# First gate and value of block 0 on three batches ahead of the fourth's output, with two loads reordered and one split

## Chip, cores, metric

One core of a Trainium2 chip. The metric is the device time of one execution in microseconds (us), the median over the executions. On one core the state is read from the times alone: slow is over 1.5% above the fastest of the same kernel, and no execution used here was. The kernel before takes 226.5 us; the change is a fine one, and everything it touches lies in the first 36 us.

## The reference, cut to what matters

```python
for b in range(nb):                       # attention in blocks, decay lam per head
    intra = einsum('bhic,bhjc->bhij', qb, kb) * Dmask
    out[:, :, sl] = einsum('bhij,bhjd->bhid', intra, vb) + einsum('bhid,bhde->bhie', qb * lam_pow, kv_state)
    kv_state = lam_block * kv_state + einsum('bhsd,bhse->bhde', kb * rev_pow, vb)
x = out.transpose(0, 2, 1, 3).reshape(B * S, H * D)          # 3072 x 512
y = (sigmoid(x @ w_gate) * (x @ w_val)) @ w_out              # d_ff 1536
```

Four batches, eight heads, 768 positions, head size 64. The kernel takes 128 positions of all four batches as one block (six blocks) and splits `d_ff` into twelve units of 128.

## The kernel before: the parts concerned

`XT` is the attention output of a block, transposed, as the input of the gate and the value. `load_w(W, src, i, w)` loads columns `i*w` to `(i+1)*w`; `GW` is 256, so `GW // 2` is one unit's slice. All loads here cast from float32 to bf16 and are issued on the POOL queue.

```python
    load(0, "v", 2, 3)
    load_w(WG, wg_r, 0, GW // 2)
    load(0, "v", 3, 4)
    load_w(WV, wv_r, 0, GW // 2)
    load_w(WG, wg_r, 1, GW // 2)
    load_w(WV, wv_r, 1, GW // 2)
    # ... (cut)
    load_gv(1, GW)                  # gate and value slices of units 2 and 3
    load_gv(2, GW)
    # ... (cut: block 0's transposes, scores, masks)
    piece_a0(1)                     # output of batch 1 into XT
    idle(2)                         # two matmuls of zeros, filler
    piece_a0(2)
    idle(2)
    g0 = psum()
    mm_part(g0, WG, 0, 0, 0, 3 * C)           # gate of unit 0 on three batches
    piece_a0(3, True)
    make_kd0(1, nc.vector)
    v0 = psum()
    mm_part(v0, WV, 0, 0, 0, 3 * C)
    mm_part(g0, WG, 0, 0, 3 * C, TCH)         # ... on the fourth
    sigm(0, 0, g0)
    mm_part(v0, WV, 0, 0, 3 * C, TCH)
    prod(0, 0, v0)
    # ... (cut) unit 1, with c(0, 0) between its gate and its value, c(0, 1) after it
    # ... units 2 and 3: both gates, both values; 4: gate, value; then 5 to 8
    t(1, 0)                         # block 1's first transposes: tq, then tk
    gv(0, 9)
    sc(1, 0)                        # block 1's first scores
```

## Time and profile before

| | before |
|---|---|
| time | 226.52 us (226.45 to 226.9) at first, 226.57 with three more executions |
| PE busy | 97% of the span of 224.5 us |
| PE idle from 36 to 222 us | 0.38 us |
| start of the first gate, end of its three-batch part | 14.68, about 15.33 us |
| start of unit 2's gate | 19.54 us |
| block 1's first `tk` transposes, last `k` load landed | 32.09, 32.07 us |

To read such a kernel, ask first where the bounding engine is not dense, then what it waits for there. A matmul busy share hides filler matmuls (the two at 13.94 us count as 0.61 us of busy time).

### The profile page before, as it was taken

Reading aid. Unit: us, or ns where it says so; the run is one execution under the profiler, and the core shown is the slowest. Engines: PE = TensorE matmul, PEld = TensorE weight load, DVE = VectorE, ACT = ScalarE, POOL = GpSimd, SP = SyncE. Lnnn points to the kernel's source line nnn. Section 1 sums busy time; section 2 is a strip of 40 time slices with the busy share of each in tenths; the row PEclk is TensorE's granted clock in tenths of the full one; section 3 lists DMA queues with packets and bytes.
Section 4 is the critical chain, followed back from the end, with each engine's and each line's share of the span. In section 5 each row is a group of like instructions: output and inputs, shape, how many; then the busy total and the mean of one; then the engine's idle time right before and its main releaser. Section 6 shows DMA issues by size and latency. Waiting matters only on the chain.

```text
span 224.5 us, 4265 instructions
## 1 busy us (share of the span) xinstructions
PE 218.5 (97%) x1748; PEld 114.6 (51%) x1748; DVE 105.5 (47%) x192; ACT 79.6 (35%) x150; POOL 78.4 (35%) x77
## 2 busy tenths in 40 slices
PE   7799999999999999999999999999999999999994
PEld 2454455888854454444445444446444445444443
DVE  7796847595530713336732445742335840333300
ACT  5664334435422234333225333115333225333221
POOL 8995698983691008930006940000000000000000
PEclk9999999999999999999999999999999999999999
DMA  6999999999999992999021999021920012100022
GB/s 109 155 173 194 189 176 156 157 194 166 157 198 184 217 178 83 204 156 108 1 96 55 230 145 133 1 96 47 176 62 0 0 53 91 47 3 0 0 93 95
DMA packets 105891, 25.70 MB, mean 114 GB/s; under 512 B 96016, under 2 KB 102928, under 8 KB 105872
## 3 DMA queue, kind: packets, MB, share of 16 engines
q0 software_dynamic: 81264, 13.90, 80.0%
q1 hardware_dynamic: 23568, 11.28, 19.7%
q10 hardware_dynamic: 1040, 0.26, 0.5%
q8 instruction: 13, 0.21, 0.4%
q14 instruction: 6, 0.05, 0.1%
HBM read 28.32 MB, written 6.29 MB: 154 GB/s over the span
## 4 chain that ended last, share of the span: by engine, by line
PE 94%; DMA 3%; DVE 1%; issue 1%; ACT 1%; POOLq 0%
PE po L478 27%; PE gp L415 21%; PE vp L421 21%; PE gp L450 5%; PE gp L429 5%; PE vp L456 5%; PE op L312 3%; PE sp L299 3%; DMA kb<-in_k_dram 3%; PE op L324 1%; PE cp L399 1%; PE po L467 1%; DVE MT L202 1%; PE tk L238 0%; ACT XT L352 0%
## 5 line engine op out<-in xcount | busy, mean ns | idle before, releaser
L424 DVE TENSOR_TENSOR ht<-sg,vp 128x512 bf16<-128x512 bf16 x54 | 37.1, 687 | 64.0 <-PE vp L421 63.9
L478 PE MATMUL po<-WO,ht 128*128 128x512 bf16 x276 | 62.0, 380 | 0.0
L415 PE MATMUL gp<-XT,WG 128*128 128x512 bf16 x216 | 55.5, 380 | 0.0
L421 PE MATMUL vp<-XT,WV 128*128 128x512 bf16 x216 | 55.4, 379 | 0.0
L418 ACT ACTIVATE sg<-gp 128x512 bf16<-128x512 f32 x54 | 32.2, 597 | 59.0 <-PE gp L415 59.0
L478 PEld LDWEIGHTS <-ht 128*128 128x128 bf16 x276 | 26.3, 98 | 31.0
L421 PEld LDWEIGHTS <-WV 128*128 128x128 bf16 x216 | 21.1, 98 | 25.5
L415 PEld LDWEIGHTS <-WG 128*128 128x128 bf16 x216 | 20.8, 98 | 24.7
L481 ACT COPY ob<-po 128x512 f32<-128x512 f32 x23 | 13.5, 585 | 52.3 <-PE po L478 50.4
L204 DVE TENSOR_TENSOR MT<-sp,mask 128x512 bf16<-128x512 f32 x40 | 25.2, 683 | 10.1 <-PE sp L299 10.1
L382 POOL TENSOR_TENSOR sd<-Sb,dec 128x512 f32<-128x512 bf16 x8 | 8.1, 1037 | 42.0 <-DVE Sb L406 42.0
L450 PE MATMUL gp<-XT,WG 128*128 128x256 bf16 x96 | 14.4, 273 | 0.0
L456 PE MATMUL vp<-XT,WV 128*128 128x256 bf16 x96 | 14.4, 273 | 0.0
L460 DVE TENSOR_TENSOR ht<-sg,vp 128x256 bf16<-128x256 bf16 x24 | 10.0, 420 | 8.6 <-PE vp L456 8.6
L453 ACT ACTIVATE sg<-gp 128x256 bf16<-128x256 f32 x24 | 9.2, 383 | 13.0 <-PE gp L450 11.9
L91 POOL DMA_DIRECT2D vb<-in_v_dram x10 | 12.8, 1281 | 0.8 <-DMA WG<-in_moe_w_gate_dram 0.6
L373 POOL TENSOR_TENSOR kd<-kb,kds 128x1024 bf16<-128x1024 bf16 x6 | 11.3, 1904 | 4.1 <-DMA kb<-in_k_dram 4.1
L406 DVE TENSOR_TENSOR Sb<-cp,sd 128x512 bf16<-128x512 f32 x8 | 5.2, 686 | 15.4 <-PE cp L399 15.4
L339 ACT CAST XT<-op 128x512 bf16<-128x512 f32 x19 | 9.9, 598 | 2.1 <-PE op L312 2.0
L450 PEld LDWEIGHTS <-WG 128*128 128x128 bf16 x96 | 9.2, 98 | 1.8 <-issue 0.2
L456 PEld LDWEIGHTS <-WV 128*128 128x128 bf16 x96 | 9.4, 98 | 1.1
L77 POOL DMA_DIRECT2D qb<-in_q_dram x8 | 9.4, 1184 | 0.0
(79 smaller groups left out, 161.7 us busy)
## 6 DMA issues: line engine op xcount, KB each, us to landing
out_dram<-ob SPq DMA_DIRECT2D x21, 256.0 KB, 2.1
kb<-in_k_dram POOLq DMA_DIRECT2D x10, 256.0 KB, 8.7
qb<-in_q_dram POOLq DMA_DIRECT2D x8, 256.0 KB, 8.3
vb<-in_v_dram POOLq DMA_DIRECT2D x4, 512.0 KB, 13.2
WO<-in_moe_w_out_dram POOLq DMA_DIRECT2D x3, 512.0 KB, 8.6
WG<-in_moe_w_gate_dram POOLq DMA_DIRECT2D x5, 256.0 KB, 8.5
WV<-in_moe_w_val_dram POOLq DMA_DIRECT2D x5, 256.0 KB, 9.0
qb<-in_q_dram POOLq DMA_DIRECT2D x6, 128.0 KB, 8.3
```

The source lines that it names most:

```text
L91: nc.gpsimd.dma_start(out=lst[n][:, b0:b1], in_=src[b0:b1, :, sl, :].rearrange("b h s d -> s (b h) d"))
L204: nc.vector.tensor_tensor(out=out.rearrange("p (e x) c -> p e x c", e=2), in0=x.rearrange("p (e x) c -> p e x c", e=2), in1=mask.rearrange ...
L373: nc.gpsimd.tensor_tensor(out=KD[n][:, e], in0=K[n][:, e], in1=kds[:, e::2].unsqueeze(1).unsqueeze(3).to_broadcast([128, B, HP, D]), op=AL ...
L415: nc.tensor.matmul(gp, lhsT=WG[:, mt, fs], rhs=x[:, mt, :], start=(mt == 0), stop=(mt == NMT - 1))
L418: nc.scalar.activation(sg, gp, AF.Sigmoid)
L421: nc.tensor.matmul(vp, lhsT=WV[:, mt, fs], rhs=x[:, mt, :], start=(mt == 0), stop=(mt == NMT - 1))
L424: nc.vector.tensor_mul(HT[n, ft], sg, vp)
L429: nc.tensor.matmul(ps[:, lo:hi], lhsT=W[:, mt, ft * 128:(ft + 1) * 128], rhs=x[:, mt, lo:hi], start=(mt == 0), stop=(mt == NMT - 1))
L450: nc.tensor.matmul(gp[:, cs], lhsT=WG[:, mt, fs], rhs=x[:, mt, cs], start=(mt == 0), stop=(mt == NMT - 1))
L456: nc.tensor.matmul(vp[:, cs], lhsT=WV[:, mt, fs], rhs=x[:, mt, cs], start=(mt == 0), stop=(mt == NMT - 1))
L478: nc.tensor.matmul(po, lhsT=HT[n, ft][:, tt * 128:(tt + 1) * 128], rhs=WO[:, ft, :], start=(ft == 0), stop=(ft == NFT - 1))
L481: nc.scalar.copy(ob, po)
```

## The change

The intent is to have PE do the gate and the value of unit 0 on three batches while the fourth batch's output is still on its way, instead of filler; to have the value slice there in time; to put the state product c(0,0) where PE waits for the copies of batch 3; and to have unit 2's gate slice land sooner, because PE would arrive at it sooner.

```diff
     load_w(WG, wg_r, 0, GW // 2)
+    load_w(WV, wv_r, 0, GW // 2)
     load(0, "v", 3, 4)
-    load_w(WV, wv_r, 0, GW // 2)
 ... piece_tk0: for the first pair of batches a PSUM tile per batch; each copy right after its four transposes
-        tk = ps_at.tile([128, 2, 2, 2 * C], BF16, name="tk", tag="ps")
 ...
+            if i == 0 or bp == 0:
+                tk = ps_at.tile([128, 1 + bp, 2, 2 * C], BF16, name="tk", tag="ps")
+            x = tk[:, i if bp else 0]
+            (four transposes into x)
+            nc.scalar.copy(KS[0, bp][:, :, i].rearrange("p e x c -> p e (x c)"), x)
 ... c(n, pair): for block 0 the copy of the state is put off
-                nc.vector.tensor_copy(dst, cp)
+                CP[bp] = cp                       # keep(bp) copies it later
 ...
-    load_gv(1, GW)
+    load_w(WG, wg_r, 2, GW // 2)
+    load_w(WG, wg_r, 3, GW // 2)
+    load_w(WV, wv_r, 1, GW)
     load_gv(2, GW)
 ...
-    piece_a0(2)
-    idle(2)
+    piece_a0(2, (nc.scalar.copy, nc.scalar.copy))     # two halves, two tiles
     g0 = psum()
     mm_part(g0, WG, 0, 0, 0, 3 * C)
-    piece_a0(3, True)
-    make_kd0(1, nc.vector)
     v0 = psum()
     mm_part(v0, WV, 0, 0, 0, 3 * C)
+    piece_a0(3, (nc.scalar.copy, nc.vector.tensor_copy))
+    make_kd0(1, nc.vector)
+    c(0, 0)
 ... (rests of gate and value as before)
+    keep(0)
 ... (c(0, 0) gone from unit 1; keep(1) after c(0, 1))
```

More of the change, by code (lines that the diff above doesn't have):

```diff
@@ L259, in piece_tk0 @@
     def piece_tk0(bp):
-        tk = ps_at.tile([128, 2, 2, 2 * C], BF16, name="tk", tag="ps")
-        for i in range(2):
-            for g in range(HP):
-                transpose_pair(tk[:, i, g // 2, g % 2 * C:g % 2 * C + C], K[0], 2 * bp + i, g)
         KS[0, bp] = trsb.tile([128, 2, 2, 2, C], BF16, tag="KS", name="KS")
         for i in range(2):
-            nc.scalar.copy(KS[0, bp][:, :, i].rearrange("p e x c -> p e (x c)"), tk[:, i])
+            if i == 0 or bp == 0:
+                tk = ps_at.tile([128, 1 + bp, 2, 2 * C], BF16, name="tk", tag="ps")
+            x = tk[:, i if bp else 0]
+            for g in range(HP):
+                transpose_pair(x[:, g // 2, g % 2 * C:g % 2 * C + C], K[0], 2 * bp + i, g)
+            nc.scalar.copy(KS[0, bp][:, :, i].rearrange("p e x c -> p e (x c)"), x)
     def piece_t(n, bp):
@@ L339, in piece_a, with piece_a0 @@
                 cp(XT[n][:, u::2, 2 * bp:2 * bp + 2, :], OP[bp, u])
-    def piece_a0(b, split=False):
+    def piece_a0(b, split=()):
         if 0 not in XT:
@@ L345, in piece_a0 @@
         for m0 in range(0, NMT, w):
-            op = ps_at.tile([128, w, C], FP32, name="op", tag="ps")
+            pool, tag = (ps_ff, "ff") if b == 2 and m0 else (ps_at, "ps")
+            op = pool.tile([128, w, C], FP32, name="op", tag=tag)
             for m in range(w):
                 intra(0, b, op[:, m, :], m0 + m, m == 0, m == w - 1)
-            if split and m0:
-                nc.vector.tensor_copy(XT[0][:, m0:m0 + w, b, :], op)
-            else:
-                nc.scalar.copy(XT[0][:, m0:m0 + w, b, :], op)
+            cp = split[m0 // w] if split else nc.scalar.copy
+            cp(XT[0][:, m0:m0 + w, b, :], op)
     def make_kd0(bp, eng):
@@ L389, in kdh, with keep @@
         return KD[n][:, b, h, :] if n == 0 else KD[n][:, h % 2, b, h // 2, :]
+    CP = {}
+    def keep(bp):
+        nc.vector.tensor_copy(Sb[:, 2 * bp:2 * bp + 2], CP.pop(bp))
     def c(n, *pairs):
@@ L561 @@
     sigm(0, 1, g1)
-    c(0, 0)
     v1 = psum()
@@ L566 @@
     c(0, 1)
+    keep(1)
     lamq_start()
```

## The prediction

> **What bounds the kernel now.** I read the page first: busy shares (part 1), the slices (part 2), the chain that ended last (part 4).
>
> ```profile
> PE 218.5 (97%) x1748; PEld 114.6 (51%) x1748; DVE 105.5 (47%) x192; ACT 79.6 (35%) x150; POOL 78.4 (35%) x77
> ...
> PE   7799999999999999999999999999999999999994
> ...
> PEclk9999999999999999999999999999999999999999
> ...
> PE 94%; DMA 3%; DVE 1%; issue 1%; ACT 1%; POOLq 0%
> ```
>
> TensorE (PE) is busy 97% of a 224.5 us span, at full granted clock, and the chain is 94% PE. The only thin slices are the first two (5.6 us each) and the last. Busy PE includes filler: line 153 multiplies zeros to keep the array occupied. So I split the span by stage (busy time of each engine in stretches):
>
> ```profile
> core 0: us, PE busy (x) PEld busy (x) DVE busy (x) ACT busy (x) POOL busy (x), PEclk, DMA share, GB/s
> 0.00:8.00 8.00, 6.22 (x28) 2.52 (x28) 5.97 (x23) 4.38 (x13) 6.94 (x11) 1.00 1.19 123
> 8.00:12.00 4.00, 2.80 (x51) 1.87 (x48) 3.25 (x7) 2.79 (x5) 4.00 (x7) 1.00 2.43 155
> 12.00:20.00 8.00, 7.87 (x103) 4.09 (x98) 7.46 (x12) 3.87 (x7) 6.31 (x10) 1.00 1.77 182
> ...
> 36.00:222.00 186.00, 185.62 (x1480) 98.35 (x1478) 79.24 (x132) 62.84 (x117) 48.73 (x40) 1.00 0.88 105
> ```
>
> From 36 us on PE misses 0.38 us of 186. No line of the change touches that work. The change can move only when PE reaches it, so its whole worth lies in 7 to 36 us. For that I read the chain in order of time there:
>
> ```profile
> 11.49 0.73 PE sp L299 x16
> 12.23 0.74 PE op L312 x16
> 12.97 0.54 PE wm L153 x2
> 13.51 0.51 PE op L312 x8
> 14.02 0.02 issue
> 14.04 0.59 ACT XT L352
> 14.64 0.04 issue
> 14.68 0.81 PE gp L429 x4
> 15.49 0.34 PE op L312 x8
> 15.83 2.07 PE gp L429 x16
> 17.90 0.37 PE cp L399 x16
> ```
>
> Read: batch 2's output `op` ends at 14.02, ScalarE (ACT) copies it into `XT` in 0.59, and only then can the first gate start at 14.68. The two filler matmuls behind batch 2 hide this wait in the busy share. From 14.68 PE is dense again to 36 us.
>
> The third reading is of the loads, because PE eats weights soon after they land. The timeline of the POOL queue shows its issues held by earlier loads:
>
> ```profile
> 22.26 0.87 POOL L85 DMA_DIRECT2D kb<-in_k_dram  x1 [0.46 <-DMA WG<-in_moe_w_gate_dram]
> 23.65 0.87 POOL L85 DMA_DIRECT2D kb<-in_k_dram  x1 [0.52 <-DMA WV<-in_moe_w_val_dram]
> ```
>
> The program's order shows eight load semaphores in rotation: a load is issued when the eighth before it has landed. The view of DMA issues, cut to single issues, gives time to landing; added to the issue's start it gives landings: `v` of batch 3 8.84 + 6.1 = 14.95, first value slice 9.71 + 6.0 = 15.7, units 2 and 3's gate slice 11.96 + 7.4 = 19.35, their value slice 12.80 + 7.8 = 20.6, units 4 and 5's value slice 14.39 + 9.0 = 23.4, and the last of block 1's first `k` loads 23.65 + 8.4 = 32.05. PE's own starts on these (timeline): 19.54, 21.07, 23.66, and about 32.26 (second half of the `tk` transposes, which begin at 32.03). So the slack is about 0.2, 0.45, 0.25 and 0.2 us. **The loads run just ahead of PE**; that is the crux.
>
> [...]
> - [...] 0.86 us per four. [...] all slices here grant full clock.
> - [...] the trace has 585 and 372, so I use the trace's.
> - [...]
> - [...] 155 GB/s while `v` loads (128 B rows) run, 0.745 us per 128 KB (176 GB/s) for 128-column weight slices, 195 GB/s for 256-column ones.
>
> **Part by part.**
>
> 1. *Batch 0 and 1's `k` transposes in a tile each.* ACT can start the first copy after four transposes (0.40 us) instead of eight (0.62): 7.92 instead of 8.15. The first mask product on VectorE (DVE) moves from 9.22 to about 9.0. But the third and fourth batches' `q` land at 10.0 and 10.85 as before, and the order shows a new wait: the fifth transpose of the second pair (one shared tile) now waits for ACT's copy of the first half, which holds `tq` of batch 2 until about 10.6. DVE ends up at 11.66 instead of 11.69 on the next product. Worth: 0 to 0.05 us.
>
> 2. *Batch 2's output in two halves, fillers gone.* First half (four matmuls) ends near 13.9. Copies of 256 columns take 0.37, the second begins about 0.3 after the first: 13.92 to 14.29 and 14.25 to 14.6. Two of the gate's four matmuls run before the second copy ends, so only two 384-column ones (0.16 each) follow: gate done at 14.97, against 14.68 + 4 x 0.16 = 15.33. Gain 0.36.
>
> 3. *Value slice ahead of the last `v`.* Value slice lands 0.85 earlier (14.85), `v` of batch 3 one half slice later: 14.95 + 0.75 = 15.70. The three-batch value part runs 14.97 to 15.62, then PE waits for `v` till about 15.78: 0.16 lost.
>
> 4. *Then.* Batch 3's output 0.34 (to 16.12); c(0,0), moved up, 0.37 (to 16.49) covers the copies of batch 3: ACT half done 16.5, DVE half about 16.3 + 0.42 = 16.72. Gate and value remainders 0.22 each with a 0.06 stall: 17.10. Then gate and value of unit 1 (0.865 each) and c(0,1) (0.37): 19.20[...]: 19.25. The kernel before starts unit 2's gate at 19.54. **Gain at unit 2: about 0.3 us.** The state copies (0.69 each) moved behind the products on DVE take nothing away: DVE has room and nobody reads `Sb` before 34 us.
>
> 5. *Unit 2's gate slice alone.* It lands near 18.0 instead of 19.35, which removes a wait that the earlier PE would meet. But two slices of 128 KB cost 2 x 0.745 = 1.49 against 262 KB / 195 = 1.34: every later load lands about 0.13 later (an estimate from the rates above).
>
> 6. *Where the gain meets the loads.* At units 4 and 5's value slice PE arrives at 23.66 - 0.3 = 23.36, data at 23.53 + 0.08: the gain shrinks to about 0.1 to 0.2. At the last `k` load PE arrives near 32.1, data at 32.05 + 0.13 + 0.05 = 32.23: 0.05 to 0.1 is left. Elsewhere slack is larger (0.8 us or more).
>
> Sum: 226.52 - 0.1, with some weight on the loads not slipping (then 0.2 to 0.3): **226.4 us**.
>
> **Rivals.**
> - *The loads do not bind.* If the order or a smaller backlog brings them as early as before, PE keeps 0.3 us or, with part 1 in full, 0.5: 226.0 to 226.2. For it: slack by my sums is only known to 0.1 us. Against: the POOL queue waits for each landing from 19 us on and the rate stays at 195 GB/s.
> - *The last `v` becomes the bound.* If it lands at 16.0 rather than 15.7, PE loses 0.3 more at batch 3's output, and the front gain vanishes: 226.5 to 226.7. For it: it moves from spare time onto the path. Against: all eight 128 KB loads there took 6.0 to 6.2 us from issue.
> - *DVE becomes the bound.* It is busy 7.46 of 8 us from 12 to 20. If batch 3's half copy comes behind a late decay product (1.22 us each), the gate's remainder waits. The order keeps copy and products as before, so I give it little; 0.2 us worse.
>
> **Range and chances.** All outcomes lie within about 0.6 us of each other, against 4.5 us for 2%. Range 225.95 to 226.85 covers the first rival at its best and the second, with the 0.2 us spread of the runs before. Faster by over 2%: 0.01; slower: 0.01; within: 0.98.
>
> **What would show it.** Right: the first gate starts near 14.3 and its four matmuls end near 15.0; batch 3's output waits for `vb` until about 15.8; unit 2's gate begins near 19.25; then new idle of PE ahead of line 434's value weights near 23.5 or of the `kb` transposes near 32.1, and the later PE work is shifted by 0.1 us. Wrong: no idle of PE at the weights or at `kb` and a shift of 0.3 or more at 36 us (loads do not bind), or a gate no earlier than before (ACT or the product on DVE holds batch 2), or a wait on DVE at batch 3's remainder.

The figures of the trace before: 0.86 us for four 512-column matmuls, the full granted clock (1.00), 585 and 372 ns for ScalarE's copies of 512 and 256 columns, and the rates of the loads. The reason given there for batch 2's output in two tiles is cut: no run has both halves in one tile, so the need for two is not shown. That the second half copy begins about 0.3 us after the first is an estimate; in the trace before two copies of 0.59 us in a row take 1.07 us together (line 352, at 12.65). In part 4 a term is cut: the recorded sum, 19.25, is 19.20 and 0.05 us for switching between weights of 64 and 128 columns. No trace shows this 0.05; before, the four matmuls ahead of c(0,1) took 0.97 us (18.20 to 19.17), where four otherwise take 0.86. Without the term the gain at unit 2 would be 0.34 us instead of 0.29. The sum at the end stays at 226.52 - 0.1 = 226.4 us: the 0.1 is what part 6 leaves at the last `k` load, by its landing, and the term is not in that.

## The result and the profile after

226.61 us (226.27 to 226.68, 6 executions) against 226.57 us for the kernel before (226.45 to 226.98, 6). The ratio is 0.9996 with a 95% interval of 0.9983 to 1.0009: the same. (Ratios are the mean time of one kernel's fast runs over that of the other's of the same rounds, so not quite the ratio of the medians.) A second series, label r_after, gave 0.9990 (0.9976 to 1.0005).

The busy shares of the page after:

```profile
PE 217.8 (97%) x1746; PEld 114.7 (51%) x1746; DVE 105.8 (47%) x192; ACT 79.8 (36%) x151; POOL 79.2 (35%) x78
```

PE has two matmuls fewer and 0.7 us less busy time, in the same span. Where the busy time went, by stage, after:

```profile
8.00:12.00 4.00, 2.71 (x47) 1.82 (x45) 3.06 (x7) 2.69 (x5) 4.00 (x6) 1.00 2.43 155
12.00:20.00 8.00, 7.52 (x103) 4.39 (x101) 7.65 (x12) 4.13 (x8) 6.65 (x9) 1.00 1.84 179
...
36.00:222.00 186.00, 185.61 (x1480) 98.40 (x1478) 79.21 (x132) 62.88 (x117) 48.93 (x40) 1.00 0.90 105
```

From 36 us on PE is as dense as before (185.61 against 185.62). The chain in order of time, after:

```profile
13.78 0.29 PE op L313 x3
14.06 0.02 issue
14.09 0.38 ACT XT L352
14.47 0.04 issue
14.51 1.46 PE gp L434 x8
15.97 0.25 PE op L313 x4
16.22 0.02 issue
16.24 0.38 ACT XT L352
16.62 0.04 issue
16.67 2.39 PE gp L434 x16
19.05 0.37 PE cp L404 x16
19.43 5.29 PE gp L434 x24
```

The front has become what was meant: behind half a copy (0.38 instead of 0.59) come eight matmuls of gate and value, not four. The part that follows c(0,1) starts at 19.43, at 19.61 before.

The first `k` load lands up to 0.2 us apart from one execution to the next, and all that follows moves with it: PE's first `tk` transpose is at 7.49 before and at 7.57 after. So I count from that transpose. Unit 2's gate then starts 12.05 us later before and 11.79 us later after (19.36): **0.26 us gained**. The start of the last output matmuls, the end of PE's work but for 2.63 us, is at 211.54 before and at 211.45 after: **0.09 us are left**. The timeline of PE and of its weight loads (PEld) shows what took the rest; before:

```profile
23.87 1.03 PE L429 MATMUL gp<-XT,WV 128*128 128x512 bf16 x4
24.73 1.03 PE L415 MATMUL gp<-XT,WG 128*128 128x512 bf16 x4
32.09 0.61 PE L280 MATMUL tk<-ident,kb 128*128 128x128 bf16 x8
```

and after:

```profile
23.54 0.68 PEld L434 LDWEIGHTS <-WV 128*128 128x128 bf16 x4 [0.19 <-DMA WV<-in_moe_w_val_dram]
23.68 1.03 PE L434 MATMUL gp<-XT,WV 128*128 128x512 bf16 x4
24.55 1.03 PE L420 MATMUL gp<-XT,WG 128*128 128x512 bf16 x4
31.90 0.78 PE L281 MATMUL tk<-ident,kb 128*128 128x128 bf16 x8
32.28 0.22 PEld L281 LDWEIGHTS <-kb 128*128 128x128 bf16 x4 [0.17 <-DMA kb<-in_k_dram]
```

The brackets are the idle time of the weight loads and what ended it. Neither wait is in the trace of before, but only one of them costs PE time. Unit 4's value weights are loaded after a wait of 0.19 us, and still the matmuls on them start 0.19 us earlier than before (23.68 against 23.87), and those of the next unit 0.18 us earlier. Before, that weight load began at 23.66, 0.21 us ahead of its matmul; after, it begins 0.14 us ahead, so the wait used up spare time only. Counted from the first transpose, every group of matmuls from unit 2's gate to the start of block 1's `tk` transposes is 0.26 us earlier than before. At these transposes the wait comes through: the eight take 0.78 us instead of 0.61, and the gate behind them starts at 32.52 on the clock, where before it started at 32.53. **These 0.17 us, at the last `k` load, are the whole loss.**

### The profile page after: what moved, and what is told of

Same layout as the page of the kernel before. It is cut to its first block, busy times and chain, and to the rows that moved or that the text cites. A ratio compares the mean times of both kernels' runs of the same rounds, so it can differ in the third digit from the quotient of the medians.

```text
span 224.5 us, 4262 instructions
## 1 busy us (share of the span) xinstructions
PE 217.8 (97%) x1746; PEld 114.7 (51%) x1746; DVE 105.8 (47%) x192; ACT 79.8 (36%) x151; POOL 79.2 (35%) x78
## 4 chain that ended last, share of the span: by engine, by line
PE 94%; DMA 3%; ACT 1%; issue 1%; DVE 0%; POOLq 0%
PE po L483 27%; PE gp L420 21%; PE vp L426 21%; PE gp L455 5%; PE gp L434 5%; PE vp L461 5%; PE sp L300 3%; PE op L313 3%; DMA kb<-in_k_dram 3%; PE op L325 1%; PE po L472 1%; PE cp L404 1%; ACT KS L267 1%; PE tk L238 1%; ACT XT L352 0%
## 5 line engine op out<-in xcount | busy, mean ns | idle before, releaser
L411 DVE TENSOR_TENSOR Sb<-cp,sd 128x512 bf16<-128x512 f32 x8 | 5.2, 686 | 15.5 <-PE cp L404 15.5
```

## The experiments

Twelve runs, each kernel timed in five rounds beside the kernel before. Every kernel was correct but for two that are wrong on purpose. The table counts from the first `tk` transpose; waits are idle times ahead of PE's weight loads from the timeline, and the number in brackets is what the wait costs PE: how much later the next matmuls start than they would by the spacing in a trace without that wait. The "lag" is worked out from the landing records in the trace: a load here raises its semaphore by 16 separate completions (in the trace after, those of the value slice of units 4 and 5 come from 21.80 to 23.50 us), and the lag is how long the last one comes behind the fifteenth, for the value slice of units 4 and 5. "Fetch" is the time that the one packet of the instruction queue between 16 and 18 us takes.

```
                unit 2's  waits for loads, 19 to 34 us   last output  lag    fetch
                gate      (of it, lost by PE)            matmuls
before          12.05     none                           211.54       0.85   948 ns
b_nok_gg        12.05     none                           211.54       0.99   948
after           11.79     value 4/5 0.19 (0.00),         211.45       0.78   948
                          k 0.17 (0.17)
r_after         11.79     value 2/3 0.20 (0.00),         211.61       0.88   948
                          4/5 0.33 (0.01), k 0.31 (0.31)
a_oldtk         11.72     value 2/3 0.32 (0.00),         211.64       0.94   948
                          4/5 0.44 (0.13), k 0.30 (0.31)
r_unsplit       12.01     gate 2/3 0.25 (0.21)           211.50       1.00   945
c_later_k       11.73     value 2/3 0.34 (0.02)          211.50       0.95   935
a_vfirst        12.48     none                           211.97       0.92   945
a_unsplit       11.79     none                           211.28       0.37   893
a_nok_gg        11.79     none                           211.28       0.28   893
d_best          11.74     none                           211.23       0.55   893
```

(The three filler runs are told below.) In both traces of the changed kernel it is the last `k` load that takes the gain; the value slices cost 0.01 us at most. No run takes the `k` wait away alone while the lag is large.

### Are the late waits what eats the gain? (a_nok_gg, b_nok_gg)

Take away what makes PE wait: the `k` transposes of block 1's first pair read `q` (wrong, relative error 0.63), and units 4 and 5 run as gate, gate, value, value.

```diff
-        turn(tk, k1)
+        turn(tk, q1)
 ...
-    g4, v4 (gate and value of unit 4), then gv(0, 5)
+    for ft in (4, 5): gate and sigmoid of ft
+    then value and product of unit 4, value and product of unit 5
```

> The changed kernel with both late waits of PE taken away: the k transposes of block 1's first pair read the q tile (wrong result on purpose, so they no longer wait for the last k load), and units 4 and 5 run as gate, gate, value, value (the value slice is needed 0.86 us later). Theory, front gain eaten by the loads: no idle of PE left between 19 and 36 us, unit 2's gate at about 19.36, the work from 36 us on about 0.2 us earlier than in the kernel before, so about 226.35 us and faster than the control by about 0.2. Rival, the front gain was never real (the 0.18 us at unit 2 is the chance of one trace): time as the control's, 226.55.

> Control: the same two edits on the kernel before, where no wait was seen at either place. Both theories: unchanged, 226.55 us within 0.1, and PE at 32.5 us where it was.

Measured: 226.34 us (ratio 0.9988, 0.9969 to 1.0007) and, for the control, 226.5 us (0.9995, 0.9978 to 1.0013). In the traces PE's last work starts at 211.28 and at 211.54: 0.26 us apart, the whole front gain, and the control is where the kernel before is. So the front gain is real and PE keeps it when it does not wait. But the run does not show that my two edits did it. In this execution the loads landed sooner than in any trace so far (the value slice of units 4 and 5 at 22.83 us, at 23.50 in the changed kernel), so PE would hardly have waited anyway. The two edits were not run apart either. That was the first sign that something else decides.

### Does a delay vanish in the waits? (a_filler, b_filler, a_fill2)

```diff
+    idle(1)            # a_filler, b_filler: one filler matmul ahead of unit 2's gate
     gs = {}
```

> The changed kernel with one filler matmul (0.22 us of PE) ahead of unit 2's gate. Theory, PE waits 0.19 us for units 4 and 5's value slice and 0.17 us for the last k load in the changed kernel: the filler only fills that waiting, PE is at the same place after the k transposes (about 32.5 us) and the time stays at 226.6, within 0.05. Rival, PE's own work sets the end from unit 2 on: 0.22 us longer, 226.8.

> The same filler in the kernel before, which had no such waits but only about 0.2 us of slack on the loads: both theories expect 0.2 us longer, about 226.75 (it needs the filler on PE's path).

Measured: 227.15 and 227.34 us, ratios 1.0017 (1.0002 to 1.0032) and 1.0033 (1.0011 to 1.0055), 0.43 and 0.62 us above the median of the kernel before in the same rounds, more than the filler's 0.22. The edit was bad. It writes the filler's PSUM tile of the first microseconds again, so that tile's buffer is not free in between, and unit 1's gate has to wait for one, as the timeline of b_filler shows:

```profile
17.35 1.02 PE L429 MATMUL gp<-XT,WG 128*128 128x512 bf16 x4 [0.46 <-ACT sg L437]
```

Before has no such wait. The pair says nothing of the theory. The second try put the filler into unit 2's own tile:

```diff
         gs[ft] = psum()
+        if ft == 2:
+            nc.tensor.matmul(gs[ft], lhsT=zero[:, :C], rhs=zero, start=True, stop=True)
```

> The filler again without its side effect (the first one kept a PSUM buffer alive and cost 0.8 us): one extra zero matmul of 0.22 us into unit 2's own gate tile, overwritten after. Theory: where PE waits at the loads (lag 0.7 us or more), the filler is absorbed and PE is at the same place after the k transposes as in the changed kernel, time 226.6; where it does not wait, 0.22 later. Rival: 0.22 us longer in any case, 226.8.

Measured: 226.67 us (six executions, 226.4 to 227.38; ratio 1.0002, 0.9986 to 1.0018), beside 226.56 us for the changed kernel on the same chip: 0.11 longer, half of the filler's 0.22, with a spread that covers both 0 and 0.22. The trace does not help. In the profiled execution (227.21 us, one of the two long ones) unit 1's value slice landed at 18.52 instead of 16.99 us, its last completion 1.50 us behind the fifteenth, and PE waited 0.60 us for it. (The same slice was as late in the trace of a_filler. In both the fetch began at 16.43 to 16.45 us, in the other traces with the large lag at 16.70 to 16.84.) Inconclusive, and told for the last point: a load can land 1.5 us late in an execution whose code ahead of it did not change.

### Did the split slice make the loads late? (a_unsplit, r_unsplit, r_after)

```diff
-    load_w(WG, wg_r, 2, GW // 2)
-    load_w(WG, wg_r, 3, GW // 2)
-    load_w(WV, wv_r, 1, GW)
+    load_gv(1, GW)
```

> The changed kernel with units 2 and 3's gate slice as one load of 256 KB again. Theory, two 128 KB slices cost 0.13 us more of the DMA engines: every later load lands about 0.13 us earlier (last k load at 32.15 instead of 32.28), unit 2's gate waits for its slice until about 19.4 to 19.5, and the wait at the k transposes shrinks to about 0.05 us; time 226.5, 0.1 us shorter or the same. Rival, the split costs nothing and the later landing was the chance of one trace: landings as in the changed kernel and time not shorter.

> The changed kernel with the gate slice in one load, once more, beside the changed kernel on the same chip. Theory: with the lag of one DMA engine at 0.7 us or more it waits too, but the loads of the other 15 engines land 0.1 to 0.2 us before those of the changed kernel, so it is 0.1 us faster or the same. Rival: the unsplit load alone removed the waits in the first trace: no waits here whatever the lag, and 0.26 us faster than the changed kernel's waiting executions.

> The changed kernel once more, to see whether its late waits depend on the execution. Theory by now: one of 16 DMA engines carries a 16 KB instruction fetch near 17 us and from then on finishes its part of every load up to 1 us after the other 15; where it is behind by 0.7 us or more, PE waits for the value slice of units 4 and 5 and for the last k load and ends its work 0.1 us before the kernel before does (both counted from the first k landing); where the lag is 0.3 us (seen in two traces), there is no wait and the end is 0.26 earlier. Unit 2's gate in either case 11.79 us after the first k transpose. Rival: the waits are the same in all executions, whatever the lag.

Measured: a_unsplit 226.47 us, ratio 0.9984 (0.9971 to 0.9998), and a trace without any wait: 0.36 us better than before in the mean, it looked like the answer. Run again beside the changed kernel on one chip it was not: r_unsplit 226.58 us (0.9996, 0.9981 to 1.001), r_after 226.56 us (0.9990). In the trace of r_unsplit unit 2's gate does wait for its slice, which lands at 19.31 us:

```profile
19.36 0.55 PEld L434 LDWEIGHTS <-WG 128*128 128x128 bf16 x4 [0.25 <-DMA WG<-in_moe_w_gate_dram]
```

So the split does what it is for: it takes this wait away. It also costs about what was predicted. In r_after and r_unsplit, whose loads up to unit 1's value slice land within 0.1 us of each other, the value slice of units 2 and 3 lands at 20.70 and 20.62 us, the last `k` load at 32.17 and 32.05: 0.08 and 0.12 us later with the split. Over all traces with the large lag, `k` lands 24.67 to 24.90 us after the first transpose with the split (seven traces) and 24.57 to 24.77 without (four), 0.15 us apart in the mean. One wait, which cost PE 0.21 us, is exchanged for three, of which the one at `k` costs 0.31, and the last output matmuls start at 211.61 with the split and at 211.50 without.

What differs between a_unsplit's two traces is not the kernel. The DMA view cut to 1.5 us, of the changed kernel (16.5 to 18) and of a_unsplit (15.5 to 17):

```profile
q0 software_dynamic: 998, 0.26, 173.1%
q8 instruction: 1, 0.02, 4.0%
```

```profile
q0 software_dynamic: 885, 0.27, 164.0%
q8 instruction: 1, 0.02, 3.7%
```

The last column is the share of 16 engines' time in the stretch. One packet of 16 KB of instructions takes 4.0% of 1.5 x 16 = 0.96 us, or 0.89 us in a_unsplit (the records have 948 and 893 ns). In the landing records of the changed kernel the last of the 16 completions comes 0.19 to 0.27 us behind the fifteenth up to this packet and 0.68 to 1.01 us behind it for the next fourteen loads. In r_after it is 0.01 to 0.03 before and 0.85 to 1.12 for the next ten. The weight load that waits for the value slice of units 4 and 5 in the changed kernel begins at 23.54 us, 0.04 after the last completion and 0.82 after the fifteenth; the one that waits for the last `k` load begins at 32.28, 0.04 after the last completion: a load counted as landed with its last here. So **the loads from 17 to 32 us are as late as the last of 16 completions, and that one falls behind when the instructions are fetched**.

Where the packet took 893 ns (three traces) the lag is only 0.28 to 0.55 us at the value slice of units 4 and 5, that slice lands 0.4 to 0.7 us earlier, and PE waits for no load from 19 to 34 us; where it took 935 to 948 ns, the lag is 0.78 us or more. The other 15 completions do not move: the fifteenth is at 22.34 us in a_unsplit and at 22.35 in r_unsplit, the last at 22.71 and 23.35. The last `k` load, the one that counts, has a lag of 0.07 to 0.37 us and lands 24.10 to 24.28 us after the first transpose in these three traces; in the others it lands at 24.57 or later. The same happens once more: in these three traces the second packet, near 33 us, takes 948 or 949 ns, and the lag goes from 0.14 to 0.34 us at the load landing then to 0.68 to 0.93 at the next; in the others it takes 936 to 975 ns, and the lag falls to 0.65 us or less. In every trace the lag is under 0.3 us up to the packet, so no completion is late by as much all the time. All this fits a packet which goes to another engine from one execution to another; the records do not name the engine, so that part is inferred. That the packet causes the lag is read from the order of events in every trace, not from taking it away: no edit of mine moves it.

### Which part does what at the front? (a_oldtk, a_vfirst)

```diff
 a_oldtk: piece_tk0 as in the kernel before
 a_vfirst:
-    load_w(WV, wv_r, 0, GW // 2)
     load(0, "v", 3, 4)
+    load_w(WV, wv_r, 0, GW // 2)
```

> The changed kernel with block 0's k transposes as before (one tile, all eight transposes ahead of the copies). Theory, the new wait of the fifth transpose of the second pair costs VectorE 0.15 us and nothing else follows because the last v load holds the batch 3 output: mask product after the q scaling at 11.7 instead of 11.85, first gate 0.1 to 0.15 us earlier, the batch 3 output still at 15.9 waiting for vb, unit 2's gate at about 19.35, time 226.6. Rival, VectorE's delay is what ate the front gain: unit 2's gate 0.15 earlier.

> The changed kernel with the last v load ahead of the value slice, as before. Theory: PE waits for the value slice (landing 15.7) with the three-batch value part until about 15.8, then needs 0.65 us for it where the changed kernel had it done: unit 2's gate 0.4 to 0.5 us later (19.8), beyond the waits of 0.36 that could hide it, so the time is 226.7. Rival, load order does not matter: 226.6 and unit 2's gate at 19.4.

a_oldtk: 226.65 us (0.9992, 0.9979 to 1.0004). The timeline of the changed kernel shows why its transposes are worth undoing. PE and then VectorE (DVE):

```profile
10.53 0.38 PE L238 MATMUL tk<-ident,kb 128*128 128x128 bf16 x4 [0.67 <-ACT KS L267]
...
11.18 0.76 DVE L256 TENSOR_TENSOR QS<-tq,lamq 128x512 bf16<-128x512 bf16 x2 [0.21 <-PE tq L238]
```

The fifth transpose of the second pair waits for a copy out of the tile that it shares, the `q` transposes behind it are late, and DVE idles 0.21 us. In a_oldtk DVE scales at 10.92 without idling, and unit 2's gate starts 0.07 us earlier (11.72). So this part of the change costs 0.07 us. It neither reached 0.15, as the rival had it, nor was it nothing, as I had expected. In the end none of it is left: in this trace PE loses 0.13 us at the value slice of units 4 and 5 and 0.31 at `k`, and ends at 211.64.

a_vfirst: 226.93 us (1.0006, 0.9994 to 1.0018). With the old order of loads the three-batch value part waits half a microsecond:

```profile
15.62 0.82 PE L434 MATMUL gp<-XT,WV 128*128 128x384 bf16 x4 [0.51 <-DMA WV<-in_moe_w_val_dram]
```

Unit 2's gate starts at 12.48, which is 0.69 us later than in the changed kernel (0.4 to 0.5 was expected), and the end at 211.97 is 0.36 later than in r_after: half of the delay vanished in waits that are no longer met (none is left in this trace), above all the 0.31 us at `k`. This is the absorption that the fillers should have shown: PE 0.69 us later at 19 us is 0.36 us later at the end.

### Versions made from this (c_later_k, d_best)

c_later_k is a_oldtk with units 4 and 5 as gate, gate, value, value, block 1's first transposes behind unit 9's gate, and the `KS` copy in halves; d_best is a_oldtk with the gate slice in one load.

```diff
 c_later_k, beside the edits shown above:
+    gate and sigmoid of unit 9
     t(1, 0)
-    gv(0, 9)
+    value and product of unit 9
     sc(1, 0)
 d_best: piece_tk0 as in the kernel before, and
-    load_w(WG, wg_r, 2, GW // 2), load_w(WG, wg_r, 3, GW // 2), load_w(WV, wv_r, 1, GW)
+    load_gv(1, GW)
```

> A version made from the theory, correct: the changed kernel with block 0's k transposes as before, units 4 and 5 as gate, gate, value, value, and block 1's first transposes put behind unit 9's gate (0.86 us later) with the KS copy in two halves. Theory: no wait for a load is left between 19 and 36 us, PE about 0.2 to 0.3 us earlier than before at 36 us, time 226.3. If the KS copy is too late for the scores, PE waits up to 0.4 us there and the time is 226.5 or more.

> A correct version from what was found: the changed kernel with one load for the gate slice and block 0's k transposes as before. Theory: unit 2's gate 0.08 us earlier than in the changed kernel (11.71 us after the first k transpose), loads 0.1 to 0.2 earlier; 226.4 in executions with the large lag, 226.15 in others. If unit 2's gate waits for its slice the gain is gone: 226.6.

c_later_k: 226.82 us (1.0002, 0.9983 to 1.002). The wait for `k` is gone (the one for the value slice of units 2 and 3 costs 0.02 us), but the scores take 0.88 us instead of 0.62 because the `KS` copy comes late, which was the expected way to fail. d_best: 226.52 us (0.9995, 0.998 to 1.0009), with the earliest end of all traces (211.23) in an execution with the smaller lag. In time neither is separable from the kernel before. No version beat both kernels clear of the noise.

## Why the prediction was right, point by point

**The number.** 226.4 us was predicted, 0.1 below before. Measured are 0.09 and 0.23 us below in the ratios of the two series, neither clear of the noise. The range held every rival as well, so a time inside it says nothing of the mechanism; the traces have to.

**The bound and the place.** Right: PE from 36 us on was untouched, and the whole effect lay before.

**Part 1, the `k` transposes** (0 to 0.05 us gained). Wrong in sign. The new wait was seen beforehand in the order of instructions, but the `q` transposes of batch 2 were put at "until about 10.6"; they began at 10.76, and DVE's next mask product came at 11.85 (11.77 with the first `k` landing as before) instead of 11.66. a_oldtk sizes the part at a loss of 0.07 us.

**Part 2, the halved copy.** The mechanism held, the term was too large: 0.36 predicted. The three-batch gate ended at 15.15 against 15.33 before, 0.25 us counted from the first transpose. The late DVE of part 1 is in it: one `op` matmul of batch 2 ran at 13.58, the next had to wait for its mask product until 13.78.

**Part 3, the last `v`.** Right in the landing, wrong in the wait: landing 15.70 and start 15.78 were predicted; it landed at 15.75 and batch 3's output started at 15.90, with `k` 0.1 later in that execution. The 0.16 us of waiting for `v` did not come about. The output starts 0.26 us after the last value matmul starts (15.64), just as before it started 0.26 us after the last gate matmul (15.16), with `v` landed since 14.95. PE came too late to wait. a_vfirst shows the alternative: 0.69 us worse at unit 2.

**Part 4, the sum at the front.** 0.3 predicted, 0.26 measured, in both traces of the changed kernel. Part of this is luck: what parts 1 and 2 fell short by took the place of the wait in part 3.

**Parts 5 and 6, the loads.** Right at the last `k` load: it takes 0.17 and 0.31 us in the two traces, and where 0.05 to 0.1 us were to be left, +0.09 and -0.07 are. Wrong at the value slice of units 4 and 5, where 0.1 us or more of the gain was to go: its weight load waits, but PE loses 0.00 and 0.01. The slack of the value slices was counted to the start of the weight loads (21.07 and 23.66); the matmuls on them started at 21.28 and 23.87, so 0.2 us more was free. The sums are loose as well: 1.49 less 1.34 is 0.15, not 0.13, and 23.61 against 23.66 would leave 0.05 us, not 0.1 to 0.2. The split's cost of 0.13 us was measured as 0.08 to 0.15.

**What the prediction did not have.** It took the landings of one trace as a property of the kernel. They are a property of the execution: they differ by up to 0.7 us, with the time that one instruction packet took. So "the loads do not bind" was not a rival to be decided. By the three traces with the smaller lag, all of other versions, it is what happens in some executions. The changed kernel's own times have one of 226.27 us in either series beside the rest at 226.5 and more, which would fit, but no profile fell on such an execution. No execution of the kernel before, in any series, is under 226.45 us, which fits too: it has no wait that could fall away. In the times the front gain is therefore mostly given back and now and then kept, which a median does not show.

**Open.** Why all kernels, the one before too, have executions some 0.4 to 1 us longer (226.9 to 227.5); and whether the instruction packet can be steered. One profile fell on a long execution of its kernel, that of a_fill2 (227.21 us, its median 226.67): there the load that landed 1.5 us late cost PE 0.60 us. Whether the others have the same cause is not shown.

## What to carry to other kernels

Where a dense engine runs just behind its loads, as PE here, an earlier start upstream can be worth no more than the slack of a later load (0.26 us were gained at unit 2, 0.17 lost again at the last `k` load): list each load's landing and its user's start before counting a gain. Take the start of the matmul, not that of its weight load, and check afterwards, group by group, where the matmuls lost their lead: idle time of a weight load is not yet time lost (0.19 us idle at the value slice of units 4 and 5, none lost). Compare traces from a common event, such as the first landing, and take a second trace of the same kernel before a load's landing is called a cause (with one load for the gate slice, that value slice landed at 22.71 us in one trace and at 23.35 in another). When a split load takes one wait away, price its smaller pieces for every load behind it (here 0.08 to 0.15 us at the last `k` load).

## What the traces show of loads and matmuls

- One 16 KB packet of instructions took 0.95 us from 16.80 us (before) and from 16.84 us (after). For the loads landed by 17.3 us the last of 16 completions was 0.27 us or less behind the fifteenth; for the 13 loads that landed next before, and the 14 after, it was 0.45 to 0.85 and 0.68 to 1.01 us behind.
- Block 0's first `k` load of 256 KB, with two loads from other queues beside it, took 6.2 us from issue to landing before, and the 128 KB loads issued from 3.7 to 11.2 us took 6.0 to 6.4 us, before and after. No load here ran alone, so no run shows what one takes by itself.
- In the trace before, casting loads ran at 155 GB/s with rows of 128 B as written (8 to 12 us), about 176 with 256 B (one 128 KB slice in 0.745 us) and 195 with 512 B (18 to 24 us): 21% and 10% less than with 512 B.
- Four 512-column matmuls, each with its weight load, took 0.86 us before (36 of them 7.77, so 216 ns for one). The granted clock in the changed kernel, without the two fillers, was 1.00 from 8 to 20 us.
